# Spectral mixing and a Mish MLP on one core: where the last block's raw w2 rows lie, and a new order of steps

## The chip, the core and the metric

The kernel runs on one core of a Trainium2 chip. TensorE multiplies matrices into PSUM; VectorE (DVE), ScalarE (ACT) and GpSimd (POOL) work on SBUF and, the first two, on PSUM; SyncE (SP) issues most of the DMAs. Each engine works through a queue of its own in the order in which the program gave it the instructions, and semaphores tie the queues together. The metric is the device time of one execution in microseconds (us), as the median of the runs.

## The reference

For x of 2048 x 512, with six modulation rows from a condition vector c:

```python
x = A_x
mod = (_silu(c) @ w_mod).reshape(c.shape[0], 6, 1, -1)
sa, ca, ga, sb, cb, gb = (mod[:, i] for i in range(6))
h = _layernorm(x, axis=-1) * (1 + ca) + sa
x = x + ga * irfft2(rfft2(h) * (w_r + 1j * w_i))
h = _layernorm(x, axis=-1) * (1 + cb) + sb
a = h @ w1 + b1                      # 512 -> 1376
x = x + gb * ((a * tanh(softplus(a))) @ w2)   # 1376 -> 512
```

The first half is a two-dimensional Fourier filter over positions and channels, the second a dense layer with Mish between two weight matrices.

## The kernel before

The work has three stages. The first takes the Fourier transform along rows and columns as matmuls with constant matrices while x streams in. The second multiplies by the filter and turns back halfway. The third, by far the longest, holds the last inverse transforms (`p3_col`, `p3_row`), the second layer norm, and the whole MLP.

In the MLP every float32 operand is split into a high part that TensorE reads exactly in its fast float32 format and a low remainder (`split`: ScalarE casts the high part, line 849, VectorE subtracts, line 850); a product then takes the three matmuls of `TERMS`.

*Up projection.* The hidden units go in five groups t = 1 to 5 of 256, and a rest t = 0 of 96 (`FL`). The 2048 positions go in four groups i of 512. For i = 1 to 3 a group (i,t) is a 2 x 2 block product done with seven unit products instead of eight; `up(i,t,j)` is unit j, six matmuls of 256 columns. `evict(i,t,j)` takes the units out of PSUM: for j = 7 ScalarE copies with the bias (line 927) and VectorE adds a second bank (line 943), for j = 2 VectorE adds (line 939), and so on; `mish_odd` and step 4 apply Mish. A later unit of the group writes into the same bank and has to wait for the eviction. The blocks of w1 come through an 8-slot ring; `fetch_w1` loads one on SP's queue when TensorE has freed its slot.

*Down projection.* The positions now go in eight blocks b = 0 to 7 of 256 (two row tiles of 128). `sums(b,t)` forms the sums that its seven-product scheme needs (VectorE, line 987), `halves(b,t,k)` splits the activations into the tiles `ah` and `al` (a ring of two; so the cast for one (b,t) waits until TensorE has read the one before the last), and `down(b,t,c)` is one piece, three matmuls. After the last piece of a block `gather(b)` copies two of its four PSUM banks (ScalarE, lines 1040 and 1041), `chain(b)` adds the banks up on VectorE (from line 1047), and `residual(b,step)` multiplies by the gate gb; for b below 7 POOL then issues a DMA that adds the result into x (line 1069), and `store(b)` sends the finished rows from x to the output (line 1078).

*The weights w2.* Tiles `w2[t]` hold the sums and splits of w2 for the seven-product scheme. The last block, b = 7, uses that scheme only for t = 1 and 2. For t = 3, 4, 5 and 0 it takes a plain product (`last_down`, and `finish` for t = 5 and 0, which also adds into x on VectorE, line 1086, and sends the last rows out, line 1087). For that it needs the raw rows of w2 once more: `load_last(ts)` loads them (`load_w2`, SP's queue, line 838) and gates them with gb at once (`gate_w2`, VectorE, line 869), and `plain_w2(t,e)` splits half e into a place that the other blocks no longer need. `split_w2(0, False)` does the same for the rest of 96.

*The order of the work.* `plan.at(key, fn, ...)` records 1150 steps with a key each, and `Plan.run` carries them out in the order of the string `ORDER`, a list of step numbers (numbered by key). The steps are issued in that order, so this string alone sets each engine's queue in the third stage: a step put early makes its engine's later instructions wait for it.

Of the kernel before, what the change touches and what calls it, by code (L numbers as in the profile page):

```python
# [7 lines left out]
F32 = mybir.dt.float32  # L8
# [4 lines left out]
P = 128  # L13
S, D, F = 2048, 512, 1376
# [5 lines left out]
NT = 6  # L20
NB = 8
# [7 lines left out]
FL = F - (NF - 1) * P  # L29
# [2 lines left out]
POOL_LOW = range(1, 15, 2)  # L32

ORDER = (
# [43 lines left out]
)  # L78


# [1 line left out]
def tile_spectral_block(ctx: ExitStack, tc: tile.TileContext, x_d, w1_d, b1_d, w2_d,  # L82
# [31 lines left out]
    def buf(tag, dt=F32):  # L114
        return work.tile([P, 512], dt, name="buf", tag=tag)
# [4 lines left out]
    x = base.tile([P, N2, D], F32, name="x")  # L120
# [567 lines left out]
    pm = ctx.enter_context(tc.tile_pool(name="pm", bufs=1))  # L688
    act = ctx.enter_context(tc.tile_pool(name="act", bufs=2))
    w2 = {}  # L690
# [140 lines left out]
    def tiles(t):  # L831
        return [(0, NF - 1, FL)] if t == 0 else [(e, 2 * t - 2 + e, P) for e in range(2)]

    def load_w2(t, spare=None):
        st["w2", t] = rs = []
        for e, f, rows in tiles(t):
            r = buf("y")[:rows] if spare is None else spare[:, e]
            nc.sync.dma_start(r, w2_d[f * P:f * P + rows, :])
            rs.append(r)
# [8 lines left out]
    def split(h, l, r):  # L848
        nc.scalar.copy(h, r)  # L849
        nc.vector.tensor_tensor(l, r, plain(h), op=ALU.subtract)  # L850
# [16 lines left out]
    def gate_w2(t):  # L867
        for r in st["w2", t]:
            nc.vector.tensor_tensor(r, r, gbr[:r.shape[0]], op=ALU.mult)

    def plain_w2(t, e):
        h, l = w2["plain", t] = [w.rearrange("p e d -> p (e d)") for w in w2[(3, 1, 2)[t - 3]]]
        split(h[:, 512 * e:512 * e + 512], l[:, 512 * e:512 * e + 512], st["w2", t][e])

    ups, acts, out_ps, done, raw = {}, {}, {}, {}, {}
# [229 lines left out]
    plan = Plan()  # L1105
# [88 lines left out]
    where = {u: k for k, u in enumerate(units)}  # L1194

    for k, (i, t, j) in enumerate(units):
# [6 lines left out]
        if (i, t) in PLAIN:  # L1203
            f, e = int(j[0][1]) - 1, int(j[1][2]) - 1
# [10 lines left out]
    start = {}  # L1215
# [74 lines left out]

    def load_last(ts):
        for t in ts:
            load_w2(t, None if t in (0, 5) else pm.tile([P, 2, D], F32, name="raw", tag="hB11" if t == 3 else "hT2"))
            gate_w2(t)

    plan.at(start[NB - 2, 4] - 4, load_last, (0,))
    plan.at(start[NB - 2, 4] + 0.3, split_w2, 0, False)
    plan.at(start[NB - 2, 4] + 0.35, load_last, (5,))
    plan.at(where[NB // 2 - 1, NT - 1, 1] + 0.6, load_last, (3,))
    plan.at(where[NB // 2 - 1, NT - 1, 6] + 0.6, load_last, (4,))  # L1300
    for t, k in ((3, start[NB - 2, 5] + 3), (4, start[NB - 1, 2]), (5, start[NB - 1, 3])):
        for e in range(2):
            plan.at(k + 0.5 + e, plain_w2, t, e)
    plan.run()
# [141 lines left out]
```

## Time and profile before

| | us |
|---|---|
| median of 3 runs | 379.63 |
| lowest, highest | 379.52, 380.19 |
| the profiled execution | 380.36 |
| its span, from the first to the last instruction | 378.6 |
| TensorE matmuls busy (PE) | 367.7 |
| weight loads busy (PEld) | 351.4 |
| VectorE busy | 305.0 |
| ScalarE busy | 251.4 |

The granted TensorE clock of the profiled execution is 0.998 of full speed. In the rows of the profile, "L914" is line 914 of the kernel before: the matmuls of `up`; L1017 are those of `down`, L1029 and L1032 those of `last_down`. Behind a tile's name stands, in brackets, how long the engine had been idle and which engine's instruction ended that. PE's end times are modelled; a busy PE column also covers small waits inside the pipeline.

### The profile page before, as it was taken

What the parts mean: (1) busy time and instruction counts of PE and PEld (TensorE: products, weight loads), DVE (VectorE), ACT (ScalarE), POOL (GpSimd) and SP (SyncE); (2) the same over time, 40 slices, a digit from 0 to 9 for tenths busy, and PEclk for the clock granted to TensorE, in tenths of its full rate; (3) what the DMA queues carried; (4) which work ended last, traced back from release to release, by engine and by line L of the source; (5) the groups of instructions that cost most, each with busy time, mean ns of one, the idle gap of its engine ahead of it and who ended that gap; (6) DMA issues with size and microseconds to landing.
All of it is one profiled execution on the core that took longest, in us unless ns stands there. A gap on an engine that the chain in (4) does not pass through costs nothing.

```text
span 378.6 us, 8181 instructions
## 1 busy us (share of the span) xinstructions
PE 367.7 (97%) x2916; PEld 351.4 (93%) x2916; DVE 305.0 (81%) x752; ACT 251.4 (66%) x553; POOL 64.8 (17%) x102
## 2 busy tenths in 40 slices
PE   8999999998999999999999999999999999999894
PEld 7999867778999999999999999999999999999894
DVE  1898968888999889999995489882677886759896
ACT  1798879995558579998757757556574553545650
POOL 0488738784000000000001000000000000000000
PEclk9999999999999999999999999999999999999999
DMA  7999987777635437668877664687664885645532
GB/s 254 342 364 375 354 344 246 249 202 275 214 138 199 139 113 230 192 242 278 282 249 168 194 169 127 166 250 221 166 219 135 241 286 190 137 154 190 160 64 103
DMA packets 44359, 81.59 MB, mean 216 GB/s; under 512 B 6784, under 2 KB 12000, under 8 KB 44064
## 3 DMA queue, kind: packets, MB, share of 16 engines
q1 hardware_dynamic: 41152, 70.46, 55.7%
q10 hardware_dynamic: 2160, 6.95, 5.9%
q0 software_dynamic: 1008, 3.67, 5.7%
q8 instruction: 23, 0.38, 0.4%
q14 instruction: 16, 0.13, 0.1%
HBM read 64.02 MB, written 13.37 MB: 204 GB/s over the span
## 4 chain that ended last, share of the span: by engine, by line
PE 87%; DVE 5%; DMA 3%; ACT 2%; SPq 1%; issue 1%; DVEq 0%; ACTq 0%
PE bank L914 27%; PE bank L1017 24%; PE bank L802 4%; PE bank L812 4%; PE bank L803 4%; PE bank L547 4%; PE bank L963 3%; PE bank L596 3%; PE bank L302 3%; PE bank L257 3%; PE bank L1013 2%; PE bank L527 2%; PE bank L768 2%; DMA xring<-in_x_t_dram 1%; DMA x<-in_A_x_dram 1%; PE bank L304 1%
## 5 line engine op out<-in xcount | busy, mean ns | idle before, releaser
L1069 POOL DMA_DIRECT2D x<-modr x7 | 6.2, 889 | 266.8 <-DVE modr L1068 110.3
L914 PE MATMUL bank<-hT,wr 128*128 128x256 f32 x360 | 51.4, 284 | 0.3 <-DVE even L939 0.3
L914 PEld LDWEIGHTS bank<-hT,wr 128*128 128x128 f32 x360 | 46.6, 191 | 0.5 <-DVE even L939 0.5
L914 PE MATMUL bank<-hB,wr 128*128 128x256 f32 x300 | 43.4, 284 | 0.1
L914 PEld LDWEIGHTS bank<-hB,wr 128*128 128x128 f32 x300 | 39.1, 191 | 0.3 <-ACT odd L927 0.3
L850 DVE TENSOR_TENSOR al<-buf,ah 128x512 fp32r<-128x512 f32 (+1 forms) x45 | 30.1, 670 | 8.6 <-ACT ah L849 8.5
L1017 PE MATMUL bank<-w2a,ah 128*128 128x256 f32 x161 | 35.3, 284 | 0.0
L1017 PE MATMUL bank<-w2b,ah 128*128 128x256 f32 x147 | 32.4, 284 | 0.0
L849 ACT CAST ah<-buf 128x512 fp32r<-128x512 f32 (+1 forms) x45 | 27.2, 607 | 6.7 <-PE bank L1017 4.5
L914 PE MATMUL bank<-hcr,wr 128*128 128x256 f32 x210 | 30.5, 285 | 0.9 <-DVE odd L943 0.6
L914 PEld LDWEIGHTS bank<-hcr,wr 128*128 128x128 f32 x210 | 27.3, 191 | 1.3 <-DVE odd L943 0.8
L1017 PEld LDWEIGHTS bank<-w2a,ah 128*128 128x128 f32 x161 | 26.8, 191 | 0.0
L802 PE MATMUL bank<-kc,d 128*128 128x128 f32 x128 | 24.9, 276 | 0.5 <-ACT d L440 0.5
L803 PE MATMUL bank<-kc,d 128*128 128x128 f32 x128 | 24.7, 275 | 0.0
L1017 PEld LDWEIGHTS bank<-w2b,ah 128*128 128x128 f32 x147 | 24.7, 192 | 0.0
L1017 PE MATMUL bank<-w,ah 128*128 128x256 f32 x112 | 21.5, 284 | 1.0 <-ACT buf L1040 1.0
L171 DVE BATCH_NORM_STATS2 st<-x 128x6 f32<-128x512 f32 x32 | 21.9, 685 | 0.2 <-DMA x<-in_A_x_dram 0.2
L776 ACT ACTIVATE buf<-bank,cols 128x256 f32<-128x256 f32 x28 | 14.1, 563 | 11.1 <-PE bank L768 11.1
L302 PE MATMUL bank<-buf,mring 128*128 128x512 f32 x48 | 20.7, 430 | 0.5 <-ACT buf L288 0.3
L802 PEld LDWEIGHTS bank<-kc,d 128*128 128x128 f32 x128 | 19.4, 192 | 0.7 <-ACT d L440 0.7
L803 PEld LDWEIGHTS bank<-kc,d 128*128 128x128 f32 x128 | 19.4, 192 | 0.0
L1017 PEld LDWEIGHTS bank<-w,ah 128*128 128x128 f32 x112 | 17.4, 191 | 1.2 <-ACT buf L1040 1.2
(288 smaller groups left out, 1092.6 us busy)
## 6 DMA issues: line engine op xcount, KB each, us to landing
wr<-w_S SPq DMA_DIRECT2D x60, 256.0 KB, 3.7
wr<-w_A SPq DMA_DIRECT2D x45, 256.0 KB, 3.4
w_S<-hT SPq DMA_DIRECT2D x20, 256.0 KB, 2.2
x<-in_A_x_dram SPq DMA_DIRECT2D x16, 256.0 KB, 5.0
xring<-in_x_t_dram SPq DMA_DIRECT2D x16, 256.0 KB, 5.0
w_A<-wr SPq DMA_DIRECT2D x15, 256.0 KB, 3.3
x<-modr POOLq DMA_DIRECT2D x7, 512.0 KB, 5.4
out_dram<-x SPq DMA_DIRECT2D x7, 512.0 KB, 4.2
```

The source lines that it names most:

```text
L171: nc.vector.bn_stats(t, x[:, n, :])
L257: nc.tensor.matmul(pgv[:, j], data(j), krs[:, j, :].rearrange("p (c q) -> p c q", c=2), start=True, stop=True)
L302: nc.tensor.matmul(pa, m[:, a, 0:128], g, start=(i == 0), stop=False)
L547: nc.tensor.matmul(pb[:, 0:w], kf[:, 0:128], z[:, 0:w], start=True, stop=True)
L776: nc.scalar.activation(dst[:, 256 * e:256 * e + 256], ps[:, 256 * e:256 * e + 256], AF.Identity, bias=cols[:, 1, 0, k:k + 1], scale=cols[: ...
L802: nc.tensor.matmul(o, dj[:, 0:128], kc[0][:, n, :], start=True, stop=False)
L803: nc.tensor.matmul(o, dj[:, 64:192], kc[1][:, n, :], start=False, stop=True)
L812: nc.tensor.matmul(px[:, j * P:(j + 1) * P], e[:, j * P:(j + 1) * P], kiv[:, j, :], start=True, stop=True)
L849: nc.scalar.copy(h, r)
L850: nc.vector.tensor_tensor(l, r, plain(h), op=ALU.subtract)
L914: nc.tensor.matmul(o, w[:, p, k, :], h[:, q, k, :], start=(first and n == 0), stop=(last and n == 5), skip_group_check=True)
L1017: nc.tensor.matmul(out_ps[b][n][:, 256 * half:256 * half + 256], a[p][:, e], w2[t][q][:, r], start=(t == 1 and half == 0 and i == 0), stop ...
```

## The change

Three things change in the program, all of them in the third stage.

Where the raw rows lie: before, t = 3 and 4 had tiles of their own named `raw`, in the places of two operand tiles of the up projection (`hB11`, `hT2`), and t = 5 and 0 used the work buffer `y`. Now they lie in x itself: rows 0 and 1 of x's second axis for t = 3, 2 and 3 for t = 4, 4 and 5 for t = 5, and the first 96 partitions of row 6 for t = 0. These rows of x belong to blocks 0 to 3 and are already stored.

Where the split parts go: before, t = 3, 4, 5 went into `w2[3]`, `w2[1]`, `w2[2]`; now into `w2[3]`, `w2[4]`, `w2[5]`. With that, t = 4 and 5 need block 6, not block 7, to be through with the place.

The order: the string `ORDER` is new from its first numbers to its last.

```diff
@@ -32,49 +32,49 @@
 ORDER = (
-    "3 1 4 2 0 16 5 21 6 15 7 26 12 73 32 75 71 38 11 9-10 8 14 13 18 52 113 80 17 82 19 22-23 47 20 24 28 105 27 "
...
-    "1135-1136 1138 1134 1129 1139 1143 1142 1132 1128 1141 1147-1148 1133 1137 1146 1149 1144 "
+    "3 1 0 14 4 2 16 21 15 5 7 6 52 8 10 123 73 12 71 17 11 13 26 118 75 19 38 32 9 44 125 24 47 80 22-23 33 18 82 "
...
+    "1138 1133 1117 1132 1145 1141 1143 1142 1144 1121 1081 1139 1147 1137 1149 1146 1148 "
 )
@@ -869,7 +869,7 @@
     def plain_w2(t, e):
-        h, l = w2["plain", t] = [w.rearrange("p e d -> p (e d)") for w in w2[(3, 1, 2)[t - 3]]]
+        h, l = w2["plain", t] = [w.rearrange("p e d -> p (e d)") for w in w2[t]]
         split(h[:, 512 * e:512 * e + 512], l[:, 512 * e:512 * e + 512], st["w2", t][e])
@@ -1290,15 +1290,14 @@
     def load_last(ts):
         for t in ts:
-            load_w2(t, None if t in (0, 5) else pm.tile([P, 2, D], F32, name="raw", tag="hB11" if t == 3 else "hT2"))
+            load_w2(t, x[:, 2 * t - 6:2 * t - 4] if t else x[:FL, 6:7])
             gate_w2(t)
 
     plan.at(start[NB - 2, 4] - 4, load_last, (0,))
     plan.at(start[NB - 2, 4] + 0.3, split_w2, 0, False)
-    plan.at(start[NB - 2, 4] + 0.35, load_last, (5,))
-    plan.at(where[NB // 2 - 1, NT - 1, 1] + 0.6, load_last, (3,))
-    plan.at(where[NB // 2 - 1, NT - 1, 6] + 0.6, load_last, (4,))
-    for t, k in ((3, start[NB - 2, 5] + 3), (4, start[NB - 1, 2]), (5, start[NB - 1, 3])):
+    for t in (3, 4, 5):
+        plan.at(where[NB // 2 - 1, t, 1] + 0.6, load_last, (t,))
+    for t, k in ((3, start[NB - 2, 0]), (4, start[NB - 2, 5]), (5, start[NB - 1, 1] + 3)):
         for e in range(2):
             plan.at(k + 0.5 + e, plain_w2, t, e)
```

In the new order the loads come as (4), (5), (3), (0), all while the last group of positions is in the up projection; before they came as (0), (3), (4), (5), the last one in the middle of block 7. `plain_w2(4)`'s first half now stands before `gather(6)`, and `split_w2(0)` just ahead of the last pieces of block 7. The keys only number the steps; where a step stands is what the string says.

82 rows, old and new, of the table ORDER are left out of this document.

## The prediction

> **What bounds the kernel now.** I read the page's table of engines first, then the windows view, the chain that ended last, and the timelines round each stop of TensorE.
>
> ```profile
> span 378.6 us, 8181 instructions
> PE 367.7 (97%) x2916; PEld 351.4 (93%) x2916; DVE 305.0 (81%) x752; ACT 251.4 (66%) x553; POOL 64.8 (17%) x102
> ```
> ```profile
> 260.00:280.00 20.00, 19.67 (x165) 19.46 (x164) 11.30 (x28) 13.80 (x31) 0.85 (x1) 1.00 0.67 194
> 280.00:300.00 20.00, 19.29 (x159) 18.88 (x158) 16.33 (x38) 10.97 (x23) 0.88 (x1) 1.00 0.58 168
> 300.00:320.00 20.00, 19.72 (x165) 19.52 (x164) 14.77 (x38) 10.04 (x22) 0.00 (x0) 1.00 0.85 278
> 320.00:340.00 20.00, 19.98 (x167) 19.78 (x167) 13.31 (x36) 9.66 (x20) 0.86 (x1) 1.00 0.47 125
> 340.00:350.00 10.00, 10.00 (x86) 10.00 (x85) 9.45 (x22) 5.39 (x12) 0.85 (x1) 1.00 0.60 200
> 350.00:360.00 10.00, 9.03 (x75) 8.83 (x75) 8.98 (x25) 6.35 (x13) 0.00 (x0) 1.00 0.58 157
> 360.00:370.00 10.00, 10.00 (x71) 9.32 (x70) 9.93 (x18) 5.32 (x10) 0.85 (x1) 1.00 0.39 99
> 370.00:378.60 8.60, 3.65 (x25) 3.04 (x23) 5.13 (x11) 0.00 (x0) 0.00 (x0) 0.89 0.20 70
> ```
>
> The columns are window, length, then the busy time of PE, PEld, DVE, ACT and POOL. TensorE bounds the kernel, so what an order of steps can win is TensorE's idle time and the tail behind its last matmul. In the windows from 260 to 360 us PE idles 0.33 + 0.71 + 0.28 + 0.02 + 0.97 = 2.31 us. From 360 on VectorE is full (9.93 of 10): it sets the end.
>
> A stop costs more than its idle time. In the chain, six matmuls of a unit of `up` take 0.72 us in a run and 0.98 just behind a stop, 0.26 more; nine matmuls of `down` take 1.08, so a piece of three takes 0.36.
>
> ```profile
> 297.71 0.98 PE bank L914 x6
> 299.05 0.72 PE bank L914 x6
> ...
> 301.21 1.08 PE bank L1017 x9
> ```
>
> TensorE's stops, with the idle time and the releaser in brackets:
>
> ```profile
> 265.80 0.98 PE L914 MATMUL bank<-hcr,wr 128*128 128x256 f32 x6 [0.33 <-DVE buf L943]
> 293.02 0.86 PE L914 MATMUL bank<-hcr,wr 128*128 128x256 f32 x5 [0.60 <-DVE odd L943]
> 316.61 0.98 PE L914 MATMUL bank<-hT,wr 128*128 128x256 f32 x6 [0.28 <-DVE even L939]
> 358.39 0.50 PE L1017 MATMUL bank<-w,ah 128*128 128x256 f32 x2 [0.97 <-ACT buf L1040]
> ```
>
> With 0.26 each (one of six records is missing at 293.02) the first three cost 0.59, 0.86 and 0.54. A fourth stands before the 0.98 row of the chain at 297.71: the window's 0.71 less 0.60 leaves 0.11, with 0.26 it is 0.37. The stop at 358.39 costs 0.97 + 0.10 (its pair took 0.50; in a run such a pair takes 0.40) = 1.07. The five make 3.43.
>
> By the Trainium skill, Perfetto Trace Analysis, Identifying the Most-Contended Engine, matmul busy time flatters TensorE and the busy share of weight loads is the better measure. By that rule the ceiling from 260 to 360 us is PEld's idle time, 0.54 + 1.12 + 0.48 + 0.22 + 1.17 = 3.53, and with all of it gone the median would be 376.1, against 377.3 by PE's 2.31. The trace agrees with the rule: the stops with their slow restarts make 3.43.
>
> How a stop arises shows best before 265.80. ScalarE's cast of `ah` sat 1.34 us waiting for TensorE to free the tile, and the eviction of the same group (L927, then L943) stood behind it, while TensorE's next unit needed the bank:
>
> ```profile
> 264.31 0.51 ACT L849 CAST ah<-odd 128x384 fp32r<-128x384 f32 x1 [1.34 <-PE bank L1017]
> 264.73 0.47 ACT L927 ACTIVATE buf<-bank,b1n 128x256 f32<-128x256 f32 x1
> ...
> 265.33 0.41 DVE L943 TENSOR_TENSOR buf<-buf,bank 128x256 f32<-128x256 f32 x1
> ```
>
> **The change, part by part.** Both orders hold the same 1150 steps, and every engine and queue issues the same number of instructions of the same shapes. Nothing is added or removed; all comes from places.
>
> *Upstream holes.* I counted TensorE work (0.72 per unit, 0.36 per piece) between each eviction's place and the unit that needs the bank. Over 15 groups and three such pairs each (step 7 to unit 3, 7 to 4, 2 to 7) ten of 45 stand within 0.36 us in the old order, three in the new.
> - 265.80 is group (2,3), 7 to 3: 0.00 before, 3.05 now. An eviction takes 0.47 + 0.41 by the rows above, so the hole closes: -0.59.
> - 316.61 is group (3,3), 2 to 7: 0.00 before, 2.52 now. -0.54.
> - 293.02 is group (2,5), 7 to 3: 0.72 before and now, but another queue ahead of it. Both ends are open, closed (-0.86, and -0.37 for the stop at 297.71 that follows in VectorE's queue) or as it is (0). I take half, -0.62, because no row decides.
> - New holes: two of the ten close places stood at a stop, so three would give 0.6 stops; at the mean of 0.59 and 0.54 that is +0.35. Bounds: 0, and all three, +1.7.
>
> Net upstream: -0.59 - 0.54 - 0.62 + 0.35 = -1.40.
>
> *The boundary into block 7.* ScalarE's queue held the cast for (7,2) ahead of the copies of `gather(6)`. That cast waits for block 6's last piece, so the copy came late:
>
> ```profile
> 357.34 0.51 ACT L849 CAST ah<-odd 128x384 fp32r<-128x384 f32 x1 [1.13 <-PE bank L1017]
> 357.76 0.58 ACT L1040 COPY buf<-bank 128x512 f32<-128x512 f32 x1
> ...
> 357.88 0.56 DVE L850 TENSOR_TENSOR al<-odd,ah 128x384 fp32r<-128x384 f32 x1 [0.84 <-ACT ah L849]
> ```
>
> Now `gather(6)` comes first, and the bank of the first copy is complete four pieces (1.44) before the block's end, that of the second two pieces (0.72): two copies of 0.58 fit. What is late next is VectorE's `chain(6)`: ahead of it stand the sums of (7,2), two splits of (7,1) and now also a low part of `plain_w2(4)`. The hole so shrinks from 1.07 to something between 0 and 1.07; VectorE, full from here, decides what it is worth, and that is counted once, in the tail.
>
> *The tail.* VectorE's work from the first sum of (7,2) to the last add of `finish`:
>
> ```profile
> 354.96 0.28 DVE L987 TENSOR_TENSOR buf<-odd 128x128 f32<-128x128 f32 x1
> ...
> 364.71 1.29 DVE L869 TENSOR_TENSOR buf<-buf,modr 128x512 f32<-128x512 f32 x2
> ...
> 373.37 0.28 PE L1032 MATMUL bank<-w2b,al 96*128 96x256 f32 x1
> ...
> 373.85 1.34 DVE L1086 TENSOR_TENSOR x<-x,bank 128x512 f32<-128x512 f32 x3
> 374.56 1.00 SPq L1087 DMA_DIRECT2D out_dram<-x  x2
> ```
> ```profile
> L850 DVE TENSOR_TENSOR w2a<-buf,w2a 128x512 fp32r<-128x512 f32 x2 | 1.4, 683 | 0.0
> L850 DVE TENSOR_TENSOR w2a<-buf,w2b 96x512 fp32r<-96x512 f32 x1 | 0.7, 679 | 0.0
> ```
>
> It runs from 354.96 to 375.19, 20.23 us, and stands still only for the 0.84 above; TensorE is done at 373.65, 1.54 before it. In the new order the two gates of `load_last(5)` (1.29) leave this stretch; the low part of `split_w2(0)` (0.68) enters it; those of `plain_w2` (683 ns each) stay in it. So -1.29 + 0.68 = -0.61, and -0.84 if nothing is waited for: -1.45 at best. The worst is +0.68: the split comes in, and the gates of (5), now in the near-full windows from 340 us on, push VectorE's whole stretch back by as much as they leave it (those of (4) and the split leave these windows, so I do not expect it). I take -1.10, near the best end, because TensorE, 1.07 earlier, would still be done before VectorE (372.6 against 374.1), and keep 0.35 for casts that wait for `ah`.
>
> *The loads and stores.* A gate follows its load at once, so VectorE holds up everything behind a late load.
>
> ```profile
> SPq L838 <- PE bank L963: 3.7, 1, 3.7
> ...
> raw<-in_B_w_dram SPq DMA_DIRECT2D x4, 256.0 KB, 2.8
> x<-modr POOLq DMA_DIRECT2D x7, 512.0 KB, 5.4
> ...
> 322.53 0.86 POOL L1069 DMA_DIRECT2D x<-modr  x1 [26.94 <-ACT ah L849]
> ...
> 341.18 12.29 SPq L1078 DMA_DIRECT2D out_dram<-x  x2
> ```
>
> The load's own wait for a tile that TensorE still reads (3.7) goes, since rows of x are long finished. What holds SP next is the fetch in front. For load (4) that fetch's slot comes free with unit 4 of (3,2): 15 pieces and 4 units, 15 x 0.36 + 4 x 0.72 = 8.3 us of TensorE work ahead of the gate's place; two issues and a landing take about 0.7 + 2.8 = 3.5. The five loads together later have 9.4. Cost 0; without that cover, 2.8 per pair. `store(4)` now stands ahead of the last fetch of a block of w1, and waits for block 4's accumulation; that was issued at 322.53 and landed some 5.4 later, 13 us before SP came to the store. Cost 0; at worst 5.4 on that fetch. `store(5)`, which held the old load (5) at 353 us, has no load behind it any more. POOL only keeps its seven accumulations.
>
> *Sum.* -1.40 - 1.10 = -2.50: the profiled execution (378.6 of span and 1.76 around it, 380.36) would take 377.86, and the median, 0.73 below it, **377.1**.
>
> **The rivals.**
> - *New holes outweigh the gains (slower).* ScalarE and VectorE work their queues in order; a cast of `ah` put too early holds back the evictions behind it, anywhere in the stage that the order covers. A stop costs 0.54 to 0.86. For slower by over 0.2% (0.76 us, about what a measurement can tell from no change) it takes 2.50 + 0.76 = 3.3, that is four stops of 0.86 or six of 0.55, among three close places and five at 0.72. Five of 0.72 give 380.7. For it: nearly every place in the stage is new. Against: only three places are closer than most old ones, and the old ten gave two stops. **0.17**.
> - *Only the tail gains.* The holes upstream move but keep their sum: 379.63 - 1.10 = 378.5. For it: (2,5) has its old distance. **0.14**.
> - *The change does nothing.* The raw rows were hidden already and VectorE's 305.0 us are the same work; the tail's gain goes into a new wait: 379.6, within 0.76. **0.11**.
> - *All holes close.* 2.36 upstream and 1.45 in the tail: 375.8. **0.05**. The rule on weight loads from the Trainium skill, Perfetto Trace Analysis, named above, puts the ceiling that high; the rows here bear it out as a ceiling, and show no order that reaches it.
>
> **How the numbers follow.** The forecast keeps 0.53, with a range of its own from 376.1 to 378.3 (both open terms, the 0.62 of (2,5) and the tail, taken to either side). Faster: 0.53 + 0.14 + 0.05 = 0.72; within 0.2%: 0.11; slower: 0.17. The range must reach to the slower case: from 375.9 to 380.3 leaves out some 0.04 below and 0.13 above.
>
> **What would show it.** Right: no PE stop released by L943 or L939 round 265 and 316 us; no ScalarE cast waiting ahead of L1040 near the end, and PE's stop there under 0.5; VectorE's last add within 1.3 us of TensorE's last matmul; no idle time before L869. Wrong: stops of 0.3 or more at other L914 or L1017 groups, VectorE idle before L869 behind a load, or the same 1.5 us between the two ends.

## The result, and the profile after

The changed kernel takes 375.49 us (median, 375.17 to 375.69) against 379.91 (379.52 to 380.54) for the kernel before, run beside it: a ratio of 0.9881, 95% interval 0.9864 to 0.9898, 4.42 us less. The prediction was 377.1 with a range down to 375.9. The sign came as forecast; the gain was 1.8 times the forecast, and the time lies below the range.

The page of the kernel after (375.52 us in the profiled execution), and its windows, with the columns of the prediction:

```profile
span 373.7 us, 8193 instructions
PE 366.8 (98%) x2916; PEld 351.8 (94%) x2916; DVE 304.8 (82%) x752; ACT 252.5 (68%) x553; POOL 65.0 (17%) x102
...
PE 91%; DVE 6%; issue 1%; ACT 0%; DVEq 0%; ACTq 0%
```
```profile
260.00:280.00 20.00, 20.00 (x170) 20.00 (x169) 10.94 (x31) 14.96 (x32) 0.00 (x0) 1.00 0.71 206
280.00:300.00 20.00, 20.00 (x169) 20.00 (x168) 18.08 (x40) 12.13 (x27) 0.88 (x1) 1.00 0.74 212
300.00:320.00 20.00, 20.00 (x169) 20.00 (x169) 12.80 (x39) 8.92 (x20) 0.00 (x0) 1.00 0.65 217
320.00:340.00 20.00, 20.00 (x170) 20.00 (x169) 17.95 (x40) 10.53 (x24) 1.39 (x2) 1.00 0.80 242
340.00:350.00 10.00, 10.00 (x85) 9.95 (x84) 8.28 (x24) 5.74 (x12) 0.33 (x1) 1.00 0.42 107
350.00:360.00 10.00, 10.00 (x82) 9.64 (x81) 9.79 (x22) 5.86 (x12) 0.10 (x1) 1.00 0.01 2
360.00:370.00 10.00, 9.61 (x62) 8.61 (x61) 9.86 (x20) 3.78 (x8) 0.76 (x1) 1.00 0.41 105
```

The engines do the same work as before. What went is idle time: from 260 to 360 us PE is busy in every window, and the chain that ended last (third line) is TensorE for 91% of the span. The two ends, in the timeline of before:

```profile
90.49 0.49 PE L802 MATMUL bank<-kc,d 128*128 128x128 f32 x2 [0.46 <-ACT d L440]
...
354.36 0.68 DVE L850 TENSOR_TENSOR w2a<-buf,w2b 96x512 fp32r<-96x512 f32 x1
...
357.14 0.28 PE L1017 MATMUL bank<-w2c,al 128*128 128x256 f32 x1
```

and of after:

```profile
90.02 0.49 PE L802 MATMUL bank<-kc,d 128*128 128x128 f32 x2 [0.46 <-ACT d L440]
...
351.50 0.29 DVE L987 TENSOR_TENSOR buf<-odd 128x128 f32<-128x128 f32 x1
...
353.28 0.57 ACT L1040 COPY buf<-bank 128x512 f32<-128x512 f32 x1
353.51 0.68 DVE L850 TENSOR_TENSOR w2b<-x,w2b 128x512 fp32r<-128x512 f32 x1
353.76 0.58 ACT L1041 COPY buf<-bank 128x512 f32<-128x512 f32 x1
354.13 0.28 PE L1017 MATMUL bank<-w2c,al 128*128 128x256 f32 x1
354.15 0.69 DVE L1047 TENSOR_TENSOR modr<-bank,buf 128x512 f32<-128x512 f32 x1
354.25 0.28 PE L1017 MATMUL bank<-w,ah 128*128 128x256 f32 x1
354.33 0.51 ACT L849 CAST ah<-odd 128x384 fp32r<-128x384 f32 x1
...
368.94 1.34 DVE L1086 TENSOR_TENSOR x<-x,bank 128x512 f32<-128x512 f32 x3
369.33 0.28 PE L1032 MATMUL bank<-w2b,al 96*128 96x256 f32 x1
```

The first matmul of line 802 opens the third stage; what lies ahead of it differs from run to run (last section), so times here count from it. VectorE's last add ends at 375.19 - 90.49 = 284.70 before and 370.28 - 90.02 = 280.26 after: -4.44, the difference of the medians. Block 6's last matmul is 266.65 after the start before and 264.11 now, -2.54 upstream. The remaining -1.90 lies behind it. The first copy of `gather(6)` (line 1040) is over 0.40 before block 7's first matmul, the second (line 1041) ends 0.09 after it, and that matmul waits for neither: it follows the last of block 6 by 0.12, the pace of matmuls of 256 columns in a run; and the last add ends 0.67 behind TensorE's last matmul instead of 1.54.

### The profile page after: what moved, and what is told of

Read it like the earlier page. It is cut to its first block, busy times and chain, and to the rows that moved or that the text cites. A ratio compares the mean times of both kernels' runs of the same rounds, so it can differ in the third digit from the quotient of the medians.

```text
span 373.7 us, 8193 instructions
## 1 busy us (share of the span) xinstructions
PE 366.8 (98%) x2916; PEld 351.8 (94%) x2916; DVE 304.8 (82%) x752; ACT 252.5 (68%) x553; POOL 65.0 (17%) x102
## 3 DMA queue, kind: packets, MB, share of 16 engines
q0 software_dynamic: 1008, 3.67, 6.0%
## 4 chain that ended last, share of the span: by engine, by line
PE 91%; DVE 6%; issue 1%; ACT 0%; DVEq 0%; ACTq 0%
PE bank L914 28%; PE bank L1017 24%; PE bank L802 4%; PE bank L812 4%; PE bank L803 4%; PE bank L547 4%; PE bank L257 4%; PE bank L963 3%; PE bank L596 3%; PE bank L302 3%; PE bank L1013 3%; PE bank L527 2%; PE bank L768 2%; PE bank L313 1%; PE bank L304 1%; PE bank L303 1%
## 5 line engine op out<-in xcount | busy, mean ns | idle before, releaser
L805 ACT COPY buf<-bank 128x512 f32<-128x512 f32 x16 | 9.4, 584 | 14.8 <-PE bank L803 14.6
```

## The experiments

All keep an `ORDER` and move single steps. A pair (a, b) in `MOVES` puts step a right ahead of step b:

```diff
+            for step, ahead_of in MOVES:
+                places.remove(step)
+                places.insert(places.index(ahead_of), step)
             assert sorted(places) == list(range(len(steps)))
```

"End" is the end of VectorE's last add after the first matmul of line 802, in each run's timeline; the median of before is that of executions beside that run.

| run | median, us | before | ratio, 95% interval | end |
|---|---|---|---|---|
| before | 379.91 | | | 284.70 |
| after | 375.49 | 379.91 | 0.9881 (0.9864 to 0.9898) | 280.26 |
| old_evict_first | 378.70 | 380.23 | 0.9962 (0.9948 to 0.9976) | 283.42 |
| old_gather_first | 380.31 | 380.23 | 1.0010 (0.9990 to 1.0029) | 284.92 |
| old_gather_chain_first | 380.18 | 380.23 | 1.0000 (0.9981 to 1.0019) | 284.52 |
| old_all_three | 378.78 | 380.23 | 0.9957 (0.9940 to 0.9973) | 283.21 |
| old_prep_first | 377.99 | 380.29 | 0.9943 (0.9926 to 0.9960) | 282.63 |
| old_order_x_rows | 381.04 | 380.08 | 1.0026 (1.0001 to 1.0052) | 285.41 |
| old_x_rows_gates_early | 380.30 | 380.29 | 0.9999 (0.9990 to 1.0008) | 284.64 |
| old_chain7_early | 379.27 | 380.25 | 0.9974 (0.9955 to 0.9994) | 283.97 |
| old_rebuilt | 378.15 | 380.29 | 0.9954 (0.9941 to 0.9967) | 283.01 |
| old_rebuilt_2 | 376.87 | 380.25 | 0.9929 (0.9905 to 0.9952) | 281.53 |
| old_rebuilt_3 | 376.42 | 380.12 | 0.9898 (0.9879 to 0.9918) | 280.89 |
| new_cast_early | 375.51 | 380.08 | 0.9865 (0.9839 to 0.9891) | 280.19 |
| new_gates_late | 376.93 | 380.08 | 0.9905 (0.9877 to 0.9934) | 281.39 |
| new_cast_7_2_first | 376.88 | 380.08 | 0.9909 (0.9878 to 0.9940) | 281.17 |
| new_chain7_late | 377.36 | 380.25 | 0.9934 (0.9912 to 0.9955) | 281.71 |
| new_pieces_old | 376.36 | 380.25 | 0.9907 (0.9886 to 0.9928) | 280.56 |
| new_order_old_places | 389.70 | 380.29 | 1.0251 (1.0235 to 1.0266) | 295.41 |
| new_order_old_places_2 | 378.96 | 380.12 | 0.9958 (0.9940 to 0.9976) | 283.05 |

Where two runs' intervals overlap, as among the "new" ones, the end and the rows tell them apart, not the medians. An end comes from one profiled execution and is good to about a quarter of a us: TensorE loses 0.24 against before in old_prep_first and old_rebuilt, 0.20 in old_chain7_early and 0.11 in old_rebuilt_3 round 181 to 186 us, ahead of every step that these runs move.

### Upstream: are the stops additive?

**old_evict_first**, the kernel before with (2,3,7), (2,5,7) and (3,3,2) earlier:

```diff
+MOVES = ((700, 704), (814, 812), (940, 901),)
```

> The kernel before with three evictions put ahead of the step that held them: (2,3,7) ahead of the cast for (3,4), (2,5,7) ahead of the cast for (4,0), (3,3,2) ahead of the residual of block 4. Theory A (every stop of TensorE costs its full price to the end, whatever VectorE does later): the stops of 0.59, 0.86 with the 0.37 that follows, and 0.54 go, -2.36 us, 377.5 against 379.9. Theory B (VectorE's work at the end sets the time and takes the gain back): 379.9, within 0.4.

Measured: 1.28 earlier at the end, -0.4% by the medians, about half of theory A's -2.36. The stops at (2,3) and (3,3) are gone, 0.59 and 0.54. Round (2,5) two stops stay, with idle times of 0.07 and 0.41; with 0.26 for the slow restart they cost 0.33 and 0.67, where 0.86 and 0.37 stood before, so 0.23 is won there (the expectation of old_prep_first has 0.23 and 0.57 for the two, which ends at the first matmul's start). 0.59 + 0.54 + 0.23 = 1.36 against 1.28: what is won upstream arrives at the last add, and VectorE's tail takes nothing back. The larger stop that stays:

```profile
296.67 0.39 PE L914 MATMUL bank<-hB,wr 128*128 128x256 f32 x1 [0.41 <-ACT odd L927]
```

**new_cast_early**: did a waiting cast stand ahead of (2,5,7)?

```diff
+MOVES = ((812, 821),)
```

> The changed kernel with one step put back: the cast for (4,0), first half, ahead of the eviction (2,5,7), where the old order had it, instead of behind. TensorE work between that eviction's place and the unit that needs the bank stays at 0.72. Theory A (a stop comes from a cast of ah that waits for TensorE ahead of the eviction, not from a short distance): a stop of 0.5 to 0.9 stands again before unit 3 of (2,5) and goes through to the end, 376.0 to 376.4 against 375.5. Theory B (other shifts of the new order closed it): no stop, 375.5.

Measured: no stop, the time of the changed kernel. Theory A fell in this form. The cast for (4,0), before and then here:

```profile
289.51 0.41 ACT L849 CAST ah<-kiv 96x256 fp32r<-96x256 f32 x1 [3.28 <-PE bank L1017]
```
```profile
287.98 0.40 ACT L849 CAST ah<-kiv 96x256 fp32r<-96x256 f32 x1
```

In the old order ScalarE stood 3.28 us before that cast with nothing to do, and the work that prepares the next positions (a cast of line 793 and the sums of line 787 behind it) piled up behind. VectorE's rows of before show it just ahead of the add that released the stop at 293.02:

```profile
291.22 0.69 DVE L794 TENSOR_TENSOR hB<-buf,hB 128x512 fp32r<-128x512 f32 x1
291.94 0.69 DVE L787 TENSOR_TENSOR buf<-buf 128x512 f32<-128x512 f32 x1
292.55 0.41 DVE L943 TENSOR_TENSOR odd<-odd,bank 128x256 f32<-128x256 f32 x1
```

In the new order that work is done earlier: ScalarE comes to the cast when TensorE has freed the tile, and the cast waits for nothing in either place.

**old_prep_first** moves that work in the kernel before:

```diff
+MOVES = ((700, 704), (940, 901), (810, 813), (816, 813), (818, 813), (814, 812),)
```

> The kernel before with the evictions (2,3,7), (3,3,2) and (2,5,7) moved as in the first run, and three steps more: the splits and the sum that prepare the next positions (split_in B21, sum_in T4, split_in T2) ahead of unit 7 of (2,5), where ScalarE and VectorE stood idle, instead of among the casts for block 4. Theory A (the stops round 293 us come from this work standing in the queues behind a waiting cast): the two stops that the first run left there, 0.23 and 0.57, go, and the time is 2.1 to 2.3 below before, some 377.8. Theory B (closing one there opens another): as the first run, 1.3 to 1.5 below before, 378.7.

Measured: 2.07 earlier at the end, 2.30 by the medians; theory A. TensorE's time lost ahead of the moved steps (0.24) accounts for the difference: without it the end is 2.31 earlier, against 2.36 for the four stops. The preparing work was not moved without the three evictions, so what it wins alone is not shown, nor does a run put it back in the new order. In its windows the 20 us with both stops are full:

```profile
280.00:300.00 20.00, 20.00 (x169) 20.00 (x168) 17.50 (x42) 11.07 (x24) 0.88 (x1) 1.00 0.67 195
```

### The boundary and the tail in the old order: every part alone wins next to nothing

**old_gather_first**, **old_gather_chain_first** and **old_all_three** (the latter with old_evict_first):

```diff
+MOVES = ((1096, 1106),)
+MOVES = ((1096, 1106), (1101, 1106),)
+MOVES = ((700, 704), (814, 812), (940, 901), (1096, 1106), (1101, 1106),)
```

> The kernel before with the two copies of gather(6) ahead of the cast for (7,2) on ScalarE; VectorE's order as before. Theory A: TensorE's stop of 1.07 before block 7 closes and all of it arrives, -1.07, 378.8. Theory B: VectorE still waits its 0.84 for that cast and its stretch of 20.23 sets the end: 379.9, within 0.4.

> The same, with VectorE's chain(6) put ahead of the cast for (7,2) too. Theory A: -1.07, 378.8. Theory B: VectorE's idle 0.84 is filled by chain(6) and its stretch gets that much shorter, -0.84, 379.1. Both say a gain here; against the run without chain(6) moved, A says the same time, B 0.84 less.

> Both edits together, five steps moved in the kernel before and nothing else. Theory A: the sums add, -2.36 - 1.07 = -3.4, 376.5, so that 1.0 of the changed kernel's 4.4 is left for the places of the raw rows and the tail. Theory B: the boundary's 0.84 alone, 379.1. If moving evictions opens new stops, each costs 0.5 to 0.9 of it.

Measured at the end: +0.22, -0.18, and -1.49, which is old_evict_first's gain and 0.21 more. The first is as theory B had it; the second is less than either theory expected. For the third, theory A had -3.4 and theory B -0.84; neither holds, and the boundary's part in it is as small as in the second. TensorE's stop did leave the boundary, and stood a little later, in the first run behind the chain's first add, in the second at a piece of (7,2):

```profile
359.13 0.36 PE L1017 MATMUL bank<-w,ah 128*128 128x256 f32 x1 [0.94 <-DVE modr L1047]
```
```profile
359.57 0.39 PE L1017 MATMUL bank<-w2a,al 128*128 128x256 f32 x1 [0.76 <-DVE al L850]
```

**old_order_x_rows**, the new places alone: the code of after with the old order of steps, `load_last(0)` behind `store(3)`.

```diff
+MOVES = ((1059, 918),)
```

> The places alone: the changed kernel's code (raw rows in x, parts in w2[3], w2[4], w2[5]) with the steps in the old order, but load_last(0) behind store(3), which sends the rows that it overwrites. Theory A (the places by themselves are worth nothing; only the order is): the time of before, 379.9, within 0.5, with the old stops. Theory B (the load's wait for a tile in use, 3.7 on SP's queue, and the gates behind it cost time): 0.6 or more below before.

Measured: 0.71 later at the end. No load waits for a tile in use any more (one waits 3.7 for the store of the rows it overwrites instead), and that is worth nothing: up to the stop below and after it TensorE keeps the pace of before. The loss is the shifted step: its gate (0.69) now stands right ahead of eviction (3,3,2), and the stop at that place grew from 0.28 to 1.00:

```profile
315.82 0.69 DVE L869 TENSOR_TENSOR x<-x,modr 96x512 f32<-96x512 f32 x1
316.43 0.41 DVE L939 TENSOR_TENSOR even<-even,bank 128x256 f32<-128x256 f32 x1
```

**old_x_rows_gates_early**: the old order on the new places, only the loads moved.

```diff
+MOVES = ((1059, 954), (1028, 1001),)
```

> Old order, raw rows in x, and one use made of it: load_last(5) with its two gates goes from the middle of block 7 to where VectorE stands idle 2.3 us at 337 us (load_last(0) stands behind eviction (3,3,2), so that its gate holds nothing). No other step moves, so all old stops stay. Theory A (VectorE's work at the end is the bound): 1.2 to 1.3 below before, 378.7. Theory B (the end of VectorE's stretch is pushed back by as much as leaves it, the worst bound of the prediction): 379.9.

Measured: no change (-0.06). Neither theory's mechanism: the gates fill an idle time at 337 us and push nothing back, and they did leave the tail, but VectorE now waits there for about as long (0.99, where they took 1.21):

```profile
364.88 0.69 DVE L850 TENSOR_TENSOR al<-buf,ah 128x512 fp32r<-128x512 f32 x1 [0.20 <-ACT ah L849]
365.49 0.69 DVE L850 TENSOR_TENSOR w2b<-x,w2c 128x512 fp32r<-128x512 f32 x1
366.96 0.69 DVE L850 TENSOR_TENSOR al<-buf,ah 128x512 fp32r<-128x512 f32 x1 [0.79 <-ACT ah L849]
```
```profile
366.31 0.62 ACT L849 CAST ah<-buf 128x512 fp32r<-128x512 f32 x1 [0.95 <-PE bank L1029]
```

The subtraction for (7,5) waits for its cast, and the cast waits for TensorE to read the tile before the last. VectorE was full in the old tail, but TensorE paced it: work that is taken out leaves a hole in front of the next cast. `chain(7)` stands behind that subtraction in the old order and ahead of it in the new one.

**old_chain7_early** and **new_chain7_late** move `chain(7)` and the first residual of block 7, in the last run's kernel and in the changed one:

```diff
+MOVES = ((1059, 954), (1028, 1001), (1130, 1117), (1133, 1117),)
+MOVES = ((1130, 1081), (1133, 1081),)
```

> The run old_x_rows_gates_early with chain(7) and the first residual of block 7 put ahead of plain_w2(5,0), so ahead of the subtraction for (7,5) on VectorE. Theory A (the gates' place gets filled only if other work of VectorE stands ahead of the casts that wait for TensorE): the idle 0.99 is filled, VectorE ends that much earlier, down to the 0.7 behind TensorE's last matmul that the changed kernel has, TensorE keeping its end: -0.85 against before, 379.3 for 380.1. Theory B (something else holds the end): no change against before.

> The changed kernel with chain(7) and the first residual of block 7 put back behind plain_w2(5,1). Theory A: VectorE stands idle some 1.2 for the cast for (7,5), and the low part of split_w2(0) comes later than TensorE needs it: +1.0 to +1.3, 376.5 to 376.8. Theory B: no change, 375.5.

Measured: -0.73 against before (-0.93 without the 0.20 lost ahead of the moved steps), the last add 0.61 behind TensorE's last matmul; and +1.45 against after, idle times of 0.63 and 0.72 ahead of those subtractions and this stop of TensorE. Theory A on both sides, the second a little dearer:

```profile
362.09 0.69 DVE L850 TENSOR_TENSOR w2b<-x,w2c 128x512 fp32r<-128x512 f32 x1 [0.63 <-ACT w2c L849]
363.51 0.69 DVE L850 TENSOR_TENSOR al<-buf,ah 128x512 fp32r<-128x512 f32 x1 [0.72 <-ACT ah L849]
...
367.97 0.50 PE L1032 MATMUL bank<-w2a,ah 96*128 96x512 f32 x1 [0.62 <-DVE w2a L850]
```

### The same parts taken out of the new order

**new_gates_late**, **new_cast_7_2_first**, **new_pieces_old**:

```diff
+MOVES = ((1028, 1134),)
+MOVES = ((1108, 1100),)
+MOVES = ((1125, 1106), (1116, 1106),)
```

> The changed kernel with load_last(5), so its two gates of VectorE, put back into the middle of block 7. The load itself finds free rows and is early enough. Theory A (VectorE, with no idle time from 350 us on, sets the end): the gates' 1.29 come back in full, 376.8. Theory B (TensorE is full to its last matmul and sets the end; the gates only fill a gap): under 0.4 more, 375.5 to 375.9.

> The changed kernel with the cast for (7,2) ahead of the copies of gather(6) on ScalarE, as in the old order. Both theories: TensorE stops about 1.0 before block 7. Theory A (VectorE sets the end): it stands idle only some 0.65 for that cast and has the subtraction done earlier in return, so +0.65, 376.1. Theory B (TensorE's stop goes through in full): +1.07, 376.6.

> The changed kernel with pieces 4 and 0 of (7,2) put ahead of pieces 1 and 6 of (7,1), as the old order mixed them. Theory A (the old mix asks for the low part of (7,2) 0.7 earlier than VectorE has it behind chain(6)): a stop of 0.5 to 0.7 there; with TensorE 0.7 ahead of VectorE at the end, +0.2 to +0.7, 375.7 to 376.2. Theory B (TensorE is the bound in full): +0.7. If the piece is not asked for too early: 375.5 and no stop.

Measured at the end: +1.13, +0.91, +0.30. In the new order, where VectorE has no wait to hide it in, each part costs. The gates' 1.28 come back nearly in full (theory A). The cast ahead of `gather(6)` brings TensorE's stop back, and VectorE's idle 0.68 with a further 0.22 later; that is between the two theories. The old mix of pieces stops TensorE 0.48 at the low part of (7,2), as theory A said. The rows of the last two:

```profile
353.89 0.51 ACT L849 CAST ah<-odd 128x384 fp32r<-128x384 f32 x1 [0.96 <-PE bank L1017]
...
354.94 0.39 PE L1017 MATMUL bank<-w,ah 128*128 128x256 f32 x1 [0.97 <-ACT buf L1040]
```
```profile
359.02 0.39 PE L1017 MATMUL bank<-w2a,al 128*128 128x256 f32 x1 [0.48 <-DVE al L850]
```

### Putting the gain together in the old order

**old_rebuilt**, **old_rebuilt_2**, **old_rebuilt_3**, all with the code of after and the old order. The first holds the moves of old_prep_first, old_x_rows_gates_early and old_gather_chain_first, and `split_w2(0)` late:

```diff
+MOVES = ((700, 704), (941, 901), (810, 813), (816, 813), (818, 813), (814, 812), (1059, 954), (1028, 1001),
+         (1100, 1108), (1104, 1108), (1081, 1147))
```

The second adds `chain(7)` with its residual, `plain_w2(4,1)` ahead of `gather(6)`, and pieces 6 and 3 of (7,1) ahead of (7,2); the third puts piece 6 behind 3, and the cast for (7,4) ahead of `gather(7)`:

```diff
-         (1100, 1108), (1104, 1108), (1081, 1147))
+         (1100, 1108), (1104, 1108), (1081, 1147), (1130, 1117), (1133, 1117), (1097, 1100), (1115, 1125), (1109, 1125))
```
```diff
-         (1100, 1108), (1104, 1108), (1081, 1147), (1130, 1117), (1133, 1117), (1097, 1100), (1115, 1125), (1109, 1125))
+         (1100, 1108), (1104, 1108), (1081, 1147), (1130, 1117), (1133, 1117), (1097, 1100), (1109, 1125), (1115, 1125),
+         (1136, 1126))
```

> Old order, raw rows in x, and eleven steps moved: the six of the run old_prep_first, the two loads of the run old_x_rows_gates_early, gather(6) and chain(6) ahead of the cast for (7,2), and split_w2(0) into the last pieces of block 7. Theory A (stops of TensorE upstream and VectorE's work at the end add up, and are all that the new order wins): 2.3 + 1.3 + 0.8 = 4.4 below before, 375.4 to 375.9, the changed kernel's time. Theory B (the rest of the new string is needed as well): 377 or more.

> The run old_rebuilt with five steps more: chain(7) and the first residual of block 7 as in the run above, plain_w2(4,1) ahead of gather(6), and the two pieces 6 and 3 of (7,1) ahead of piece 4 of (7,2). Sixteen steps of the old order are moved in all. Theory A (these are the parts that the new string wins by): 4.2 to 4.5 below before, 375.6 to 375.9. Theory B (more of the string is needed): 376.5 or more, with a stop or an idle time left that names it.

> The run old_rebuilt_2 with piece 6 of (7,1) behind piece 3, and the cast for (7,4) ahead of gather(7). Theory A (its two remaining waits are what is left): 0.6 to 0.9 below that run, 376.0 to 376.3, VectorE without an idle time above 0.3 and TensorE without a stop above 0.3. Theory B (the waits were not on the path): 376.9.

Measured at the end: -1.69, -3.17, -3.81, of 4.44. The first fell 0.38 short of old_prep_first alone, so its tail moves won nothing: theory B, and what it lacked stands in its rows, a stop of 0.78 at (7,2) and idle times of 0.41 and 0.79 ahead of two casts. The second was short by 1.3, again named by its rows (a stop of 0.45; VectorE's idle 0.66 for the cast of (7,4)). The third comes within 0.63 of the changed kernel, 0.34 of it upstream of block 7 (block 6's last matmul is at 264.45, not 264.11). So seventeen moved steps of 1150, on the new places, carry most of the gain. The starts of TensorE's matmuls give nearly all of the remaining 0.63. Upstream this run loses 0.28 at 321.72 us, 0.06 at 313.87 and 0.11 ahead of the moved steps, where after loses 0.10 at 346.45. In block 7 it loses 0.46 at two places, where after loses 0.19. By its end the third run is theory A (0.64 below the second); by the medians it is 0.45. The stop of the second run:

```profile
356.99 0.39 PE L1017 MATMUL bank<-w,ah 128*128 128x256 f32 x1 [0.45 <-DVE modr L1055]
```

### The new order without the new places

**new_order_old_places** and **new_order_old_places_2**: the code of before in the new order, in its own step numbers, with six steps moved to where the old tiles allow them; the second differs in the two loads (1043 and 1079) alone.

```diff
+MOVES = ((1043, 1053), (1078, 1102), (1121, 1120), (1117, 1120), (1079, 1124), (1129, 1133))
```
```diff
-MOVES = ((1043, 1053), (1078, 1102), (1121, 1120), (1117, 1120), (1079, 1124), (1129, 1133))
+MOVES = ((1043, 1071), (1078, 1102), (1121, 1120), (1117, 1120), (1079, 1134), (1129, 1133))
```

> The new order with the places of before: raw tiles in hB11 and hT2 and the buffer y, so load_last(4) has to stand behind unit 6 of (3,5), split_w2(0) ahead of block 7, load_last(5) and the halves of plain_w2(4) and (5) in block 7; all other steps as in the new order. Theory A: nothing stops upstream, but the gates (1.29) and the first half of plain_w2(4) (0.6) stand in VectorE's last stretch again: 1.2 to 1.9 above the changed kernel, 376.7 to 377.4. Theory B (the places are worth nothing once the order is right): 375.5 to 375.9.

> The new order with the places of before, load_last(5) now ahead of store(6) and load_last(4) behind the last fetch of w1. Theory A (the places let gates and one half of plain_w2(4) leave VectorE's last stretch, and that is their worth): 1.2 to 1.9 above the changed kernel, 376.7 to 377.4. Theory B (the places are worth nothing once the order is right): 375.5 to 375.9.

Measured: the first ends 10.7 later than before. Load (5) stood behind `store(6)` on SP's queue, which waits for block 6's accumulation, and VectorE behind the load; upstream TensorE stopped 1.40 for a fetch of w1 and 1.94 for an eviction that stood behind the gates of (4), which waited 1.92 for their load:

```profile
370.06 0.34 SPq L1078 DMA_DIRECT2D out_dram<-x  x1
370.49 1.21 SPq L838 DMA_DIRECT2D buf<-in_B_w_dram  x2
```
```profile
373.78 1.35 DVE L869 TENSOR_TENSOR buf<-buf,modr 128x512 f32<-128x512 f32 x2 [6.46 <-DMA buf<-in_B_w_dram]
```

It tells nothing of A or B. Nor is the 10.7 the price of the late loads alone: the granted clock, 1.00 in every other run from 10.1 us to TensorE's last matmul, was 0.50 here from 350.2 to 353.6 us, 1.4 after the idle time of 1.94, and from 374.1 to 384.4, from within one of 4.67 on. Behind the columns of the prediction stands the granted clock, before the last two:

```profile
344.00:346.00 2.00, 2.00 (x19) 2.00 (x18) 0.42 (x1) 0.56 (x2) 0.00 (x0) 1.00 0.92 192
350.00:352.00 2.00, 2.00 (x12) 1.96 (x11) 2.00 (x5) 0.83 (x2) 0.00 (x0) 0.56 0.26 104
380.00:382.00 2.00, 2.00 (x6) 1.57 (x5) 1.93 (x4) 0.00 (x0) 0.00 (x0) 0.50 0.00 0
```

In these stretches matmuls of 256 columns start 0.21 apart instead of 0.12, and those of 512 columns 0.43 instead of 0.23; by their starts this cost about 3.5 us. PE is busy for 2.00 of 2.00 in all three windows, so its busy column does not show the lower clock. Whether the idle times brought it is not shown: no run varies them.

The second ends 2.79 above after, more than theory A's 1.2 to 1.9: the gates of (5) are back in the tail, and those of (4), now late, bring a stop of 0.42 ahead of block 7. So the places alone win nothing (old_order_x_rows, old_x_rows_gates_early), the order on the old places wins 1.65 with these six steps where they are (another placing of two of them lost 10.7), and both 4.44.

## Why the prediction was wrong

Its signs all came: no stop behind L943 or L939, no waiting cast ahead of the copies of `gather(6)`, no stop of TensorE before block 7, the last add 0.67 behind the last matmul, no idle time before a gate. The terms were too small, and what failed is the step that priced upstream holes by the distance between an eviction and the next unit, with the allowances for waits in the tail:

- *265.80 and 316.61, -0.59 and -0.54*: right, and old_evict_first shows that they pass to the end.
- *(2,5), half of 0.86 + 0.37 "because no row decides"*: closed in full, 0.62 missed. The step failed because it looked at the distance to the next unit alone. What stands in the queues ahead decided here, and the trace had the row: ScalarE's 3.28 us before the cast for (4,0), with the preparing work behind it. By old_prep_first, moving that work closes what was left there. (The prediction takes one record to be missing at 293.02. None is: its view ended inside the unit, and a longer one has all six matmuls, 0.98 us, so the 0.86 holds.)
- *New holes, +0.35 from ten close places with two stops*: none came; no row of TensorE in the stage shows idle time, also at the three close places. Distance was no measure here either.
- A short stop at 324.68 (the starts round it lose 0.28) was not in the list; it closed too, and after loses 0.10 at 346.45 instead, so 0.18 in all. Together 0.62 + 0.35 + 0.18 = 1.15: upstream -2.54 instead of -1.40.
- *358.39, 1.07*: too small for TensorE. The matmul starts 1.25 behind the one before, where 0.12 is a run's pace, and its pair takes 0.10 more: 1.23. This did not enter the sum, which counted the boundary in the tail.
- *The tail, -1.45 best, -1.10 taken*: the stretch from the first sum of (7,2) to the last add is 370.28 - 351.50 = 18.78 against 20.23, so -1.45, the best end. The 0.35 kept for waiting casts was not needed.
- *"The low part of split_w2(0) enters it", +0.68*: charged, but its leaving the place right ahead of the stretch was not credited. In the old trace it stands at 354.36, and the first sum follows at once. After, VectorE reaches that sum 0.45 earlier against block 6's last matmul. That the moved split brought this is read from the two queues; no run moves it alone.

0.62 + 0.35 + 0.18 + 0.35 + 0.45 = 1.95, and -2.50 - 1.95 = -4.45. The rival "all holes close" (375.8, chance 0.05) is what came, and it too lacked the 0.18 and the 0.45.

One reason was wrong where its number was nearly right. "From 360 on VectorE is full: it sets the end" took a full engine for the bound. In the old order the gates could leave it without a gain (old_x_rows_gates_early), as could TensorE's stop (old_gather_first): TensorE, the ring-of-two casts and VectorE held one another. The tail's -1.45 needs the gates out, `gather(6)` ahead of the cast, `chain(7)` ahead of (7,5), and the pieces unmixed, and the prediction named only the first two: that its best end came out to the hundredth was luck.

The ceiling by weight loads (the Trainium skill, Perfetto Trace Analysis, Identifying the Most-Contended Engine) came nearer than PE's idle column, but was passed. By the Trainium skill there, matmul busy time is no good measure of how close TensorE is to its limit; that it flatters is the prediction's word, which this trace bears out. PEld idled 3.53 from 260 to 360 us before and 0.41 after; PE idled 2.31 before. TensorE reaches block 7's first matmul at 264.23 instead of 267.90, 3.67 earlier. The prediction's check of the rule, stops of 3.43, was partly chance: with 1.23 for the last stop and the 0.28 at 324.68 they make 3.87. As a ceiling of the whole it was lower still, since it leaves out what follows TensorE's last matmul: there another 0.87 went (1.54 to 0.67).

## What to carry to other kernels

Where an engine works its queue in order, look for the instruction that waits longest and ask what stands behind it; the distance between a producer and its consumer says little (ten close places gave two stops before, three gave none after). An engine that is full at the end is not yet the bound: if its work is cut to the pace of another engine, taking some out only makes the wait visible, so price such a part together with what could move up into its place. A storage change and an order can be worth nothing and 1.7 alone and 4.4 together. A stop costs more than the idle time that the trace shows for it (0.26 more for a unit of `up` here), so read it from the starts of the matmuls.

## What the runs showed that was not expected

The scatter between executions (379.0 to 382.2 for the kernel before, in the 34 executions beside old_evict_first) was larger than most of these effects, and at least part of it lies ahead of the changed stage. The first matmul of line 802 came between 89.65 and 92.24 us in twenty profiled executions whose first two stages are the same work. The windows from 5 to 10 us of after, where it came at 90.02, and of new_pieces_old, 92.17:

```profile
5.00:10.00 5.00, 5.00 (x40) 5.00 (x39) 1.81 (x6) 0.11 (x1) 0.00 (x0) 1.00 1.03 358
```
```profile
5.00:10.00 5.00, 5.00 (x26) 5.00 (x26) 0.00 (x0) 0.00 (x0) 0.00 (x0) 1.00 0.97 335
```

Both show PE busy for 5.00 of 5.00 us at a granted clock of 1.00, with 40 matmuls (358 GB/s moved) and with 26 (335 GB/s): in this stretch a full PE column doesn't show that matmuls came more slowly, and the column of weight loads, 5.00 in both, doesn't either; the count of instructions does. That they waited for loads is likely, not shown.
